# One attention and feed-forward kernel: the loads of q, k and v from the eighth pair on, moved from SyncE's queue to GpSimd's

## The chip, the cores and the metric

The kernel runs on one core of one Trainium2 chip. The metric is the device time of one execution in microseconds, given as the median of several runs. A core has five engines with an instruction queue each: TensorE (PE, matmuls; its weight loads are listed as PEld), VectorE (DVE), ScalarE (ACT), GpSimd (POOL) and SyncE (SP). Transfers (DMA) can be issued from the queues of SP, ACT and POOL; the core's 16 DMA engines carry them all. In the profile, SPq stands for SP's queue.

## What is computed

Attention over 8 batches of 8 heads with 1152 keys of 64 elements. The queries are first averaged in twos, so 576 are left. Behind it stands a feed-forward part without an activation function.

```python
batch, n_heads, seq, head_dim = (8, 8, 1152, 64)
...
q_pool = q.reshape(B, H, S // factor, factor, D).mean(axis=3)
scores = scale * np.matmul(q_pool, k.transpose(0, 1, 3, 2))
...
attn = np.exp(scores)
attn = attn / (np.sum(attn, axis=-1, keepdims=True) + 1e-09)
return np.matmul(attn, v).astype(np.float32)
...
a = x @ w1
b = x @ w2
h = a * b @ w3
return (h @ w_out).astype(np.float32)
```

Here x is the attention's result with the heads side by side: 4608 rows of 512. Inputs and output are float32. w1 and w2 are 512 x 1024, w3 is 1024 x 1024 and w_out is 1024 x 512.

## The kernel before

**Pairs.** Two heads of one batch form a pair; there are NP = 32 pairs, numbered from 0. For each pair the kernel loads k into kst, the queries into qst and a small rest of them into qtl (`load_kq`, L327, L330, L331), and v into vst (`load_v`, L337). Each of these tiles has two buffers, so the load of pair p needs the cast of pair p-2 to be done with its buffer.

**Casts, on POOL.** `cast_kq` turns k to float16 (L343) and adds neighbouring queries (L347, L349) into kq16, of which there are two. `cast_v` writes the values as float16 into vaug (L356), of which there are five.

**Turning.** Scores need keys and queries with the head's elements along the partitions. For pairs 1 to 7 TensorE turns kq16 (`transp_pe`, L371). From pair 8 on a DMA transpose on SP's queue does (`transp`, L363), into kqT, of which there are three. A DMA transpose on the same queue also turns the attention's results of pairs 8 to 31 (xb) into xT (`x_dma`, L473).

**Work on TensorE.** The scores of all pairs form one long row that is cut into 324 groups of 512 columns, three groups to a "visit". `scores` (L431) computes a group, and ACT takes the exponential (L436) into a ring. The product with the values (L459, L462) follows in units of 128 queries; DVE normalises (L483, L497). Between them stand matmuls of the feed-forward part as filling: first w3 times w_out, turned into one matrix T16 (L535, L544), then, as soon as 512 rows of x are there, the two projections (L566) and the product with T16 (L610). Its result goes through DVE (L620) into osb, of which there are three, and is stored to the output (`store`, L574, L578) from POOL's queue; in the tail of the kernel from SP's and ACT's. Each 512 rows make four such results.

**Order.** The order of instructions on each engine is the order in which the program names them; it is written out at build time. A planner (`_visits`) chooses what TensorE does between the scores of two visits, from a model of TensorE, ACT and DVE alone. While the scores of pair pn begin, the program names `transp(pn + 1)` and then `prepare(pn + 2)`. So on POOL the casts of pair p are followed by whatever `prepare(p)` issues from POOL, and then by the stores that come due.

**The loads' queues.** `prepare(p)` casts pair p's keys and queries and pair p-1's values, and then loads the values of pair p and the keys and queries of pair p+2. For p below 8 it issues these loads from POOL, from 8 on from SP. The loads before the first `prepare` go through several queues and the weights' loads through POOL's.

Of the kernel before, what the change touches and what calls it, by code (L numbers as in the profile page):

```python
# [255 lines left out]
def kernel(  # L256
# [11 lines left out]
    nc = tc.nc  # L268
# [55 lines left out]
    def load_kq(p, k_eng, q_eng):  # L324
        b, h0 = p // HP, 2 * (p % HP)
        kst = att.tile([128, 2, NJ * D], FP32, tag="kst")
        k_eng.dma_start(out=kst, in_=k[b, h0:h0 + 2].rearrange("u (p c) d -> p u (c d)", p=128))  # L327
        qst = att.tile([128, 2, QM * 2 * D], FP32, tag="qst")
        qtl = att.tile([QT, 2, 2 * D], FP32, tag="qtl")
        q_eng.dma_start(out=qst, in_=q[b, h0:h0 + 2, 0:QM * 256].rearrange("u (p c) d -> p u (c d)", p=128))  # L330
        q_eng.dma_start(out=qtl, in_=q[b, h0:h0 + 2, QM * 256:S].rearrange("u (p t) d -> p u (t d)", t=2))  # L331
        kq[p] = (kst, qst, qtl)

    def load_v(p, eng):
        b, h0 = p // HP, 2 * (p % HP)
        vst = att.tile([128, 2, NJ * D], FP32, tag="vst")
        eng.dma_start(out=vst, in_=v[b, h0:h0 + 2].rearrange("u (p c) d -> p u (c d)", p=128))  # L337
        vs[p] = vst

    def cast_kq(p):  # L340
        kst, qst, qtl = kq.pop(p)
        kq16 = kq16s[p % 2]
        nc.gpsimd.tensor_copy(out=kq16[:, 0:NJ].rearrange("p c u d -> p u c d"),  # L343
                              in_=kst.rearrange("p u (c d) -> p u c d", d=D))
        qv = qst.rearrange("p u (c t d) -> p u c t d", t=2, d=D)
        eng = nc.gpsimd
        eng.tensor_tensor(out=kq16[:, NJ:NJ + QM].rearrange("p c u d -> p u c d"),  # L347
                          in0=qv[:, :, :, 0], in1=qv[:, :, :, 1], op=ALU.add)
        eng.tensor_tensor(out=kq16[0:QT, NJ + QM], in0=qtl[:, :, 0:D], in1=qtl[:, :, D:2 * D], op=ALU.add)  # L349
        pairs[p] = kq16  # L350

    def cast_v(p):
        va = vaugs[p % NVA]
        if p < NVA:
            nc.gpsimd.memset(va[:, :, :, D:E1], 1.0 / SCL)
        nc.gpsimd.tensor_copy(out=va[:, :, :, 0:D], in_=vs.pop(p).rearrange("p u (c d) -> p u c d", d=D))  # L356
# [307 lines left out]
    def w3_load(r):  # L664
        nc.gpsimd.dma_start(out=w3c[r // 2][:, 2 * (r % 2):2 * (r % 2) + 2, :],
                            in_=moe_w3[256 * r:256 * r + 256, :].rearrange("(c p) f -> p c f", p=128))

    def w_load(dst, src):
        nc.gpsimd.dma_start(out=dst, in_=src.rearrange("(c p) f -> p c f", p=128))
# [24 lines left out]
    load_kq(3, nc.gpsimd, nc.gpsimd)  # L694

    def prepare(p):
        early = p < 8
        cast_kq(p)
        cast_v(p - 1)
        eng = nc.gpsimd if early else nc.sync  # L700
        load_v(p, eng)
        if p in (2, 3):
            w3_load(p)
        if p == 4:
            w_load(w1sb, moe_w1)
        if p == 5:
            w_load(w2sb, moe_w2)
        if p + 2 < NP:
            load_kq(p + 2, eng, eng)
# [13 lines left out]
    for c in range(B * Sq // CH):  # L723
        n = 0
        for b in range(B):
            for t in range(NT5):
                if xpos(b, t) < (c + 1) * CH and xpos(b, t) + (128 if t < QM else QT) > c * CH:
                    p = b * HP + HP - 1
# [44 lines left out]
    for vis in range(NVIS):  # L773
        if vis == T_START:
            queue.append(t_groups())
        for s in range(vis * VS, vis * VS + VS):
            pn = (s * G + G - 1) // FLAT
            if pn != seen:
                seen = pn
                if pn == 0:  # L780
                    first_turn(0, K0, turn_bank(), nc.scalar.copy)
                    first_turn(NJ, NJ + QM, avb.bitcast(FP16), nc.vector.tensor_copy, nc.scalar.copy)
                if NPE <= pn + 1 < NP:
                    transp(pn + 1)
                if 0 < pn < NP - 2:
                    prepare(pn + 2)
                elif pn + 2 == NP:
                    cast_v(NP - 1)
            scores(s)
            if s == 0:  # L790
                first_turn(NB - 1, NB, turn_bank(), nc.vector.tensor_copy)
        if vis == 0:
            first_turn(K0, NJ, turn_bank(), nc.vector.tensor_copy)
            prepare(2)
        for what in order[vis]:
            if what == "P":
                transp_pe(turn[vis].pop(0))
            elif what == "A":
                av_step()
            else:  # L800
                assert fill(what == "s")
# [67 lines left out]
```

## Time and profile before

| | us |
|---|---|
| median of three runs | 414.98 |
| lowest and highest of them | 414.73, 415.25 |
| span of the profiled execution | 414.1 |
| first score matmul | 7.1 |
| last score matmul ends | 346.6 |
| SP waiting before transposes of results (L473) for DVE | 49.1 + 44.3 in the two largest groups |
| vst, kst, qst: issue to landing from SP's queue, median | 4.9, 5.9, 7.2 |
| the same from POOL's queue | 7.2, 9.8, 10.4 |

The span runs from the first instruction to the end of the last one of the profiled execution; a run's time has a little around it. DMA time is read in two parts: the issue, which occupies the queue that issues it, and the landing, which is when its semaphore is complete. Packets of SP's queue (q1 in the profile) take 59.1% of the 16 DMA engines' span, those of POOL's queue (q0) 21.6%.

### The profile page before, as it was taken

The numbers are of one execution on the slowest core, as the hardware profiler recorded it, in microseconds if no ns is written. First come the engines' busy times: TensorE is split into PE (matmuls) and PEld (weight loads), VectorE is DVE, ScalarE is ACT, GpSimd is POOL, SyncE is SP. The second block draws the span as 40 slices with busy tenths as digits, with TensorE's granted clock in tenths as the row PEclk, the third lists the DMA queues.
The fourth block names the chain that finished last, engine by engine and source line by source line (L and its number), as shares of the span: only waits on it lengthen the run. The fifth ranks groups of instructions, "written<-read, shape, count | busy, mean of one in ns | idle before, by whom it ended". The sixth has DMA issues, their size and how long they took to land.

```text
span 414.1 us, 12744 instructions
## 1 busy us (share of the span) xinstructions
PE 399.9 (97%) x5337; PEld 246.9 (60%) x5337; DVE 205.5 (50%) x573; ACT 323.4 (78%) x353; POOL 167.6 (40%) x212
## 2 busy tenths in 40 slices
PE   3899999999999999999999999999999999999995
PEld 1477787565556655566556556655777655644442
DVE  1256665665356535554455436553556346744241
ACT  4878979898989998899999999999899986022321
POOL 4979976470655316504535155505532210010000
PEclk9999999999999999999999999999999999999999
DMA  8999999999799898959999999998975440030302
GB/s 263 210 320 289 269 286 312 348 247 265 185 238 252 221 286 278 242 70 278 273 264 280 264 252 270 292 260 163 303 207 121 85 90 15 16 114 2 101 0 108
DMA packets 90832, 86.34 MB, mean 209 GB/s; under 512 B 59664, under 2 KB 64272, under 8 KB 90768
## 3 DMA queue, kind: packets, MB, share of 16 engines
q1 hardware_dynamic: 81312, 58.80, 59.1%
q0 software_dynamic: 8880, 25.63, 21.6%
q10 hardware_dynamic: 576, 1.05, 0.8%
q8 instruction: 42, 0.69, 0.7%
q14 instruction: 22, 0.18, 0.1%
HBM read 67.11 MB, written 9.44 MB: 185 GB/s over the span
## 4 chain that ended last, share of the span: by engine, by line
PE 93%; ACT 2%; DMA 2%; DVE 1%; issue 1%; SPq 0%; POOL 0%; ACTq 0%
PE psc L431 20%; PE avb L462 17%; PE mot L566 16%; PE mo L566 15%; PE mo L610 11%; PE mot L610 5%; PE mo L544 3%; PE avb L459 3%; ACT ring L436 2%; PE ptk L371 2%; DMA kst<-in_k_dram 2%; DVE kqT L373 1%; PE mot L544 1%; PE mo L535 1%; PE mot L535 1%
## 5 line engine op out<-in xcount | busy, mean ns | idle before, releaser
L436 ACT ACTIVATE ring<-psc 128x1024 f16<-128x1024 f32 x324 | 308.3, 1025 | 33.8 <-PE psc L431 32.0
L462 PEld LDWEIGHTS <-ring 128*128 128x128 f16 x2304 | 84.4, 98 | 26.3 <-issue 7.1
L431 PE MATMUL psc<-kqT 64*128 64x512 f16 (+7 forms) x1152 | 96.2, 291 | 3.4 <-ACT ring L436 0.9
L462 PE MATMUL avb<-vaug,ring 128*128 128x65 f16 x2304 | 91.4, 193 | 0.0
L343 POOL CAST kq<-kst 128x1152 f16<-128x1152 f32 x31 | 35.7, 1150 | 74.3 <-DMA kqT<-kq 52.3
L431 PEld LDWEIGHTS <-kqT 64*128 64x128 f16 x1152 | 46.0, 95 | 31.0 <-issue 8.4
L578 POOL DMA_DIRECT2D out_dram<-osb x23 | 12.7, 551 | 101.6 <-DVE rzall L483 99.9
L610 PE MATMUL mo<-T,gT 128*128 128x512 f16 x192 | 45.6, 380 | 0.0
L566 PEld LDWEIGHTS <-w2sb 128*128 128x128 f16 x320 | 28.2, 98 | 28.3 <-issue 4.2
L566 PEld LDWEIGHTS <-w1sb 128*128 128x128 f16 x320 | 28.2, 98 | 27.7 <-issue 3.9
L610 PEld LDWEIGHTS <-gT 128*128 128x128 f16 x280 | 25.3, 98 | 32.2 <-issue 5.2
L483 DVE RECIPROCAL rzall<-avb 128x2 f32<-128x2 f32 x144 | 23.8, 165 | 37.0 <-PE avb L462 20.2
L566 PE MATMUL mot<-xT,w1sb 128*128 128x512 f16 (+2 forms) x172 | 41.1, 364 | 0.1
L620 DVE TENSOR_SCALAR osb<-mo 128x512 f32<-128x512 f32 x24 | 16.6, 692 | 48.5 <-PE mo L610 48.5
L347 POOL TENSOR_TENSOR kq<-qst 128x512 f16<-128x512 f32 x31 | 39.4, 1272 | 1.2 <-DMA qst<-in_q_dram 1.2
L566 PE MATMUL mot<-xT,w2sb 128*128 128x512 f16 (+2 forms) x156 | 38.0, 368 | 0.0
L356 POOL CAST vaug<-vst 128x1152 f16<-128x1152 f32 x32 | 36.6, 1143 | 2.6 <-DMA vst<-in_v_dram 2.5
L599 DVE TENSOR_TENSOR gT<-mot,asb 128x512 f16<-128x512 f32 x37 | 25.6, 692 | 22.0 <-PE mot L566 20.8
L599 DVE TENSOR_TENSOR gT<-mo,asb 128x512 f16<-128x512 f32 x35 | 24.2, 692 | 24.6 <-PE mo L566 24.4
L566 PE MATMUL mo<-xT,w2sb 128*128 128x512 f16 (+2 forms) x164 | 36.2, 349 | 0.0
L595 DVE COPY asb<-mo 128x512 f32<-128x512 f32 x32 | 22.1, 691 | 24.0 <-PE mo L566 23.7
L566 PE MATMUL mo<-xT,w1sb 128*128 128x512 f16 (+2 forms) x148 | 33.1, 351 | 0.0
(76 smaller groups left out, 287.4 us busy)
## 6 DMA issues: line engine op xcount, KB each, us to landing
vst<-in_v_dram SPq DMA_DIRECT2D x25, 576.0 KB, 4.9
kst<-in_k_dram SPq DMA_DIRECT2D x23, 576.0 KB, 5.9
qst<-in_q_dram SPq DMA_DIRECT2D x23, 512.0 KB, 7.2
out_dram<-osb POOLq DMA_DIRECT2D x23, 256.0 KB, 5.2
kst<-in_k_dram POOLq DMA_DIRECT2D x8, 576.0 KB, 9.8
qst<-in_q_dram POOLq DMA_DIRECT2D x8, 512.0 KB, 10.4
vst<-in_v_dram POOLq DMA_DIRECT2D x7, 576.0 KB, 7.2
w3c<-in_moe_w_dram POOLq DMA_DIRECT2D x4, 512.0 KB, 8.1
```

Of the source, the lines that this page charges most:

```text
L343: nc.gpsimd.tensor_copy(out=kq16[:, 0:NJ].rearrange("p c u d -> p u c d"), in_=kst.rearrange("p u (c d) -> p u c d", d=D))
L347: eng.tensor_tensor(out=kq16[:, NJ:NJ + QM].rearrange("p c u d -> p u c d"), in0=qv[:, :, :, 0], in1=qv[:, :, :, 1], op=ALU.add)
L356: nc.gpsimd.tensor_copy(out=va[:, :, :, 0:D], in_=vs.pop(p).rearrange("p u (c d) -> p u c d", d=D))
L431: nc.tensor.matmul(psc[:, u, f - s * G:f - s * G + ln], kT2[u * 64:u * 64 + 64, jt, :], qpT[u * 64:u * 64 + 64, i0:i0 + ln], start=True, s ...
L436: nc.scalar.activation(out=ring[:, :, r0:r0 + G], in_=psc, func=AF.Exp, bias=0.0, scale=SCALE)
L462: nc.tensor.matmul(avb[:, o + u * E1:o + u * E1 + E1], ring[:, u, c0:c0 + 128], va[:, u, jt, :], start=(jt == 0 and u == 0), stop=(jt == N ...
L483: nc.vector.reciprocal(out=rzall[:, i, :], in_=av[:, :, D:E1].rearrange("p u o -> p (u o)"))
L566: nc.tensor.matmul(pw[:, d0:d0 + n], wt[:, mc, ft * 128:ft * 128 + 128], xT[:, mc, a:a + n], start=(mc == 0 and d0 == 0), stop=(mc == NC - ...
L595: nc.vector.tensor_copy(out=t["a"], in_=pa)
L599: nc.vector.tensor_tensor(out=t["g"][:, ft, :], in0=pb, in1=t["a"], op=ALU.mult)
L610: nc.tensor.matmul(po, t["g"][:, ft, tt:tt + 128], T16[:, ft, :], start=(ft == 0), stop=(ft == NF - 1))
L620: nc.vector.tensor_scalar_mul(out=osb, in0=po, scalar1=1.0 / (SCL * SCL))
```

## The change

In `prepare`, the variable `early` goes, and all loads that this function issues go through POOL's queue.

```diff
     def prepare(p):
-        early = p < 8
         cast_kq(p)
         cast_v(p - 1)
-        eng = nc.gpsimd if early else nc.sync
+        eng = nc.gpsimd
         load_v(p, eng)
         if p in (2, 3):
             w3_load(p)
...
         if p + 2 < NP:
             load_kq(p + 2, eng, eng)
```

For p from 8 to 31 the load of the values, and for p from 8 to 29 the three loads of keys and queries of pair p+2, stand on POOL behind the casts of the same call. On SP's queue, after the loads of the start, the DMA transposes of kq16 and of xb are left, and the stores of the tail. Sizes, buffers and everything on TensorE, DVE and ACT stay as they are.

## The prediction

> **What bounds the kernel now.** I read the page's head first, then the stretch in which the changed loads act, then the waits, then the two queues that trade work.
>
> The page's first part, and the busy time of each engine from 90 to 346 us (from the first pair whose loads move until the last score matmul):
>
> ```profile
> span 414.1 us, 12744 instructions
> ...
> PE 399.9 (97%) x5337; PEld 246.9 (60%) x5337; DVE 205.5 (50%) x573; ACT 323.4 (78%) x353; POOL 167.6 (40%) x212
> ```
>
> ```profile
> 90.00:346.00 256.00, 255.68 (x3676) 158.34 (x3675) 130.04 (x364) 234.20 (x247) 97.96 (x113) 1.00 0.93 222
> ```
>
> In that stretch (columns: length, then busy us of PE, PEld, DVE, ACT, POOL; granted clock, DMA share, GB/s) TensorE is idle for 256.00 - 255.68 = 0.32 us, at a granted clock of 1.00. No load ends a TensorE wait there. So a better feeding of the data can win at most 0.3 us, and POOL, which gets the new work, is idle for 158 us.
>
> Whom the waits name, and the groups of POOL (busy us, mean ns of one, then idle time before it and its releaser):
>
> ```profile
> POOL out_dram L578 <- DVE rzall L483: 99.9, 18, 25.7
> POOL kq L343 <- DMA kqT<-kq: 52.3, 9, 12.6
> ```
>
> ```profile
> L347 POOL TENSOR_TENSOR kq<-qst 128x512 f16<-128x512 f32 x31 | 39.4, 1272 | 1.2 <-DMA qst<-in_q_dram 1.2
> L356 POOL CAST vaug<-vst 128x1152 f16<-128x1152 f32 x32 | 36.6, 1143 | 2.6 <-DMA vst<-in_v_dram 2.5
> L343 POOL CAST kq<-kst 128x1152 f16<-128x1152 f32 x31 | 35.7, 1150 | 74.3 <-DMA kqT<-kq 52.3 <-issue 11.8 <-PE ptk L371 5.7
> L349 POOL TENSOR_TENSOR kq<-qtl 64x128 f16<-64x128 f32 x31 | 14.0, 450 | 0.0
> L578 POOL DMA_DIRECT2D out_dram<-osb x23 | 12.7, 551 | 101.6 <-DVE rzall L483 99.9 <-DVE osb L620 1.7
> L330 POOL DMA_DIRECT2D qst<-in_q_dram x8 | 5.8, 728 | 0.0
> L327 POOL DMA_DIRECT2D kst<-in_k_dram x8 | 5.8, 726 | 0.0
> L337 POOL DMA_DIRECT2D vst<-in_v_dram x7 | 5.1, 726 | 0.0
> L331 POOL DMA_DIRECT2D qtl<-in_q_dram x8 | 4.9, 610 | 2.3 <-DMA wosb<-in_moe_w_out_dram 1.3 <-DMA w1sb<-in_moe_w_dram 1.0
> ```
>
> POOL mostly waits for results to store or for a transpose to have read the buffer that the next cast writes. The last four rows are the price of issuing on POOL what is to move.
>
> **The change part by part.** In the two programs' instruction orders, PE, DVE and ACT keep theirs. 90 issues leave SP and join POOL: 24 of vst (pairs 8 to 31) and 22 each of kst, qst and qtl (pairs 10 to 31).
>
> *POOL's time.* By the rows above a pair's four issues take 0.726 + 0.726 + 0.728 + 0.610 = 2.79 us. In all 24 x 0.726 + 22 x 2.064 = 62.8 us, so POOL goes from 167.6 to about 230 us (56%). A pair's casts take 1.150 + 1.272 + 0.450 + 1.143 = 4.02 us, and the 29 stores (15.9 us) come to 0.66 us a pair. A round is then 4.02 + 2.79 + 0.66 = 7.5 us. The pairs go by at (336.7 - 106.2) / 22 = 10.5 us, from the first score matmul of pair 9 to that of pair 31. POOL keeps 3 us a round. On the path that sets the end: 0.
>
> *What stands behind the new issues on POOL.* The next store or the next cast comes up to 2.8 us later. Here the cover counts, which I took pair by pair from the trace's landing times and first uses. The transposed keys kqT land 3.0 to 12.3 us before the first score matmul that reads them. The tightest are pairs 17, 18 and 19 (3.2, 3.0, 3.5 us). These three are held by SP's queue, not by POOL: the cast of pair 18 was done at 173.6, yet its transpose is issued at 187.74. The value tiles vaug are ready 18 to 36 us early.
>
> *SP's queue.* It loses 90 issues of 0.4 to 0.6 us, and what they blocked:
>
> ```profile
> 182.58 2.57 SPq L363 DMA_TRANSPOSE kqT<-kq  x1
> 185.24 0.54 SPq L337 DMA_DIRECT2D vst<-in_v_dram  x1
> 185.87 0.41 SPq L327 DMA_DIRECT2D kst<-in_k_dram  x1
> 186.38 0.42 SPq L330 DMA_DIRECT2D qst<-in_q_dram  x1
> 186.89 0.76 SPq L331 DMA_DIRECT2D qtl<-in_q_dram  x1
> 187.74 4.83 SPq L363 DMA_TRANSPOSE kqT<-kq  x1
> ```
>
> Pair 18's transpose waits here only for the issues before it; with these gone it follows pair 17's by about 185, 2.5 us earlier. Its 4.83 us (the shortest of the 24 took 1.53) I read as a ring still full of loads. All that is earlier feeds an engine with 0.3 us of idle time: 0 to -0.3 us, taken as 0.
>
> *The transfers.* Moved loads share the 16 DMA engines with the transposes as before, only from another ring. Landing on POOL's queue took a median of 7.2 us (vst), 9.8 (kst) and 10.4 (qst) against 4.9, 5.9 and 7.2 on SP's, but the POOL ones ran beside the weights, up to 1 MB each. The last set, clear of them (issued from 70.77), took 5.5, 6.7, 8.3 and 7.9 us. Bounds for the moved loads: 4.9 to 10.8 us for vst (slowest on POOL), 5.9 to 13.8 for kst. I take the last set, the nearest in kind. A kst or qst is issued two rounds ahead, 2 x 10.5 - 6.8 = 14 us before its cast: covered at all but the slowest qst seen (14.7). A vst is issued one round ahead; the round holds while it lands within 10.5 - 1.1 = 9.4 us: covered, except at the bound.
>
> *Placing POOL's issue against DVE.* The moved issues took 0.71 to 0.75 us each for kst in the first 75 us, when DVE worked most. In the stretch in question no DVE instruction takes over 0.69 us, so if each issue waited for a whole one, a round is 7.5 + 4 x 0.69 = 10.2 us, still under 10.5.
> The Trainium skill speaks against the change here: "SBUF — State Buffer", section "A bandwidth-pool intuition that's wrong", has a GpSimd-issued DMA of about 0.62 us take about 3.1 us beside a VectorE copy that holds the port the two share. By that figure a round would be some 17 us and the kernel some 150 us slower, an estimate from that page alone; the trace, with 31 load issues all near their usual length, does not agree.
>
> **Sum:** span 414.1 + 0. The median of the three runs (414.98) lies 0.9 us above this execution's span and moves with it: 415.0 us, own range 414.4 to 415.6 (0.3 us of idle time and the runs' spread of 0.5).
>
> **The rivals.**
>
> *A, slower: POOL's own load loop becomes the bound.* Place: from a vst issue through its landing to the cast at L356 and the next vst issue, all on POOL in order. It decides once vst lands later than 9.4 us. At the slowest 10.8 a round is 10.8 + 1.1 = 11.9 us: 24 x 1.4 = 34 us, less some 9 us of kqT cover, about 440. For it: three of seven POOL vst took 8.7 us or more. Against: these ran beside weights; the one clear set took 5.5.
>
> *B, slower by little: a store late enough to hold its buffer.* osb has three buffers and each group of output rows writes four. Only the group stored from 193.81 has casts just before it (to 191.1); the new issues fill 191.1 to 193.9, and its first store queues behind 1.7 MB of loads. It landed at 200.18; the fourth osb is written at 202.25. If it lands 9 to 10.4 us after the loads' last issue, plus a little for itself, that is 203 to 205. DVE is then 1 to 3 us late, of which 1.1 us (osb's end at 202.94 to the next matmul on that bank at 204.01) is free: 415.0 to 416.8.
>
> *C, slower: the transposes lose their place.* In one ring an earlier transpose precedes later loads; in two rings they mix. If pair 17's transpose, issued at 182.6 because of DVE and not of the loads, landed after the longest time seen (11.2 us), it would be at 193.8 against a first use at 190.4: +3.4, so 418.4. The same place has xT for the chunk projected from 204.0: landed 204.5, read by the fourth matmul at 204.66. Against: both sat behind loads in one ring before.
>
> *D, slower: the issue itself is blocked by DVE* (above): over 10.5 us a round needs more than 0.75 us lost at each issue; at 1 us each, (11.5 - 10.5) x 24 = 24 us, about 439.
>
> *E, faster:* 0.3 us idle is all there is. A gain over 0.8 us needs TensorE itself to run faster while fewer loads sit in SP's ring: nothing in the rows speaks for it. 414.0 at most.
>
> That the change doesn't move the loads is excluded by the instruction orders.
>
> **How the numbers follow.** Forecast 0.74, A 0.05, B 0.09, C 0.08, D 0.01, E 0.03. About 0.2% (0.8 us) is what this measurement can tell from no change. Half of B stays within it: same 0.74 + 0.05 = 0.79, slower 0.04 + 0.05 + 0.08 + 0.01 = 0.18, faster 0.03. The range takes the forecast's own low end, and reaches past B, 416.8, to 417.0; C, A, D and E lie outside (0.17).
>
> **What would show it.** Right: POOL near 230 us busy, TensorE's idle time from 90 to 346 under 1 us, SP's kqT transposes issued in nearer 1.5 than 3.6 us, kqT of pairs 17 to 19 earlier. Wrong: a wait of score matmuls for the kqT transposes (C), of POOL's L356 for vst in most rounds (A), of DVE's L620 for a store (B), or POOL issues of over 1 us (D).

## The result, and the profile after

The changed kernel takes a median of 438.87 us (four runs, 434.31 to 447.81), beside 414.94 us for the kernel before on the same chip. The ratio is 1.0535, with a 95% interval of 1.0502 to 1.0567: slower by 5.4%, where 415.0 us was forecast. The ratio, like each one below, leaves out runs over 1.5% above the fastest of the same kernel, here the one of 447.81. The runs also differ by 13.5 us among themselves; those of the kernel before lie within 0.5 us.

The head of the page of the profiled execution (438.53 us), with the row of granted clock and that of GB/s from its 40 slices of 10.9 us:

```profile
span 436.8 us, 12622 instructions
...
PE 405.6 (93%) x5337; PEld 249.5 (57%) x5337; DVE 205.7 (47%) x573; ACT 323.5 (74%) x353; POOL 229.4 (53%) x302
...
PEclk9999999999999999999689999999988999999999
...
GB/s 276 266 302 327 290 297 253 220 222 216 249 300 210 228 248 245 297 120 237 119 161 232 252 226 238 253 271 223 251 208 127 93 87 38 14 110 1 98 0 102
```

The loss of 22.7 us of span has two parts. TensorE's time without work grew from 414.1 - 399.9 = 14.2 to 436.8 - 405.6 = 31.2 us, by 17.0. Its busy time grew by 405.6 - 399.9 = 5.7 us for the same 5337 matmuls: the clock row falls to 6 and 8 tenths in places. POOL is busy for 229.4 us, where about 230 was worked out. In the slice from 207.5 to 218.4 us the DMA engines move only 119 GB/s, although transfers are waiting, as the stretch below shows.

Who waited, in the list of waits (us in total, times, longest):

```profile
POOL kq L343 <- DMA kqT<-kq: 55.7, 8, 13.8
...
PE psc L431 <- DMA kqT<-kq: 10.1, 3, 6.1
...
DVE osb L620 <- DMA out_dram<-osb: 8.6, 1, 8.6
...
PE avb L462 <- DVE xb L497: 7.4, 2, 6.5
POOL vaug L356 <- DMA vst<-in_v_dram: 5.9, 6, 2.3
```

The two PE rows hold 10.1 + 7.4 = 17.5 us, which is about the new idle time (17.0). The first is a wait for turned keys. In the second TensorE waits for DVE's L497, which in turn stood behind L620 and its wait for a store.

The list of transfers (line, queue, count, KB each, median us from issue to landing) of the changed kernel:

```profile
vst<-in_v_dram POOLq DMA_DIRECT2D x31, 576.0 KB, 6.1
kst<-in_k_dram POOLq DMA_DIRECT2D x30, 576.0 KB, 7.7
qst<-in_q_dram POOLq DMA_DIRECT2D x30, 512.0 KB, 9.2
out_dram<-osb POOLq DMA_DIRECT2D x23, 256.0 KB, 8.1
```

and its transposes there, then the stores and the same two in the list of the kernel before:

```profile
kqT<-kq SPq DMA_TRANSPOSE x24, 9.7
xT<-xb SPq DMA_TRANSPOSE x24, 6.9
```

```profile
out_dram<-osb POOLq DMA_DIRECT2D x23, 256.0 KB, 5.2
...
kqT<-kq SPq DMA_TRANSPOSE x24, 6.6
xT<-xb SPq DMA_TRANSPOSE x24, 4.8
```

In the median the loads landed near what was forecast for them (5.5, 6.7 and 8.3): the moved ones alone have 6.2, 7.1 and 8.5, the slowest of them 14.5, 15.2 and 17.5. What nobody moved got late: kqT from 6.6 to 9.7 us, with a longest of 28.9 instead of 11.2 us, xT from 4.8 to 6.9, the stores from 5.2 to 8.1.

**One stretch, step by step.** POOL, SP's queue and the end of DVE's wait around the first large hole, from the timeline (start us, us, then in brackets the idle time before it and its releaser). POOL:

```profile
190.92 1.15 POOL L343 CAST kq<-kst 128x1152 f16<-128x1152 f32 x1 [9.86 <-DMA kqT<-kq]
...
194.73 0.72 POOL L337 DMA_DIRECT2D vst<-in_v_dram  x1
...
196.89 0.60 POOL L331 DMA_DIRECT2D qtl<-in_q_dram  x1
197.48 1.12 POOL L578 DMA_DIRECT2D out_dram<-osb  x2
...
208.92 0.60 POOL L331 DMA_DIRECT2D qtl<-in_q_dram  x1 [1.80 <-DMA qtl<-in_q_dram]
...
224.68 1.15 POOL L343 CAST kq<-kst 128x1152 f16<-128x1152 f32 x1 [13.79 <-DMA kqT<-kq]
```

SP's queue:

```profile
195.71 6.60 SPq L363 DMA_TRANSPOSE kqT<-kq  x1
212.18 1.19 SPq L473 DMA_TRANSPOSE xT<-xb  x1
213.47 11.09 SPq L363 DMA_TRANSPOSE kqT<-kq  x1
```

DVE and PE:

```profile
209.32 0.69 DVE L620 TENSOR_SCALAR osb<-mo 128x512 f32<-128x512 f32 x1 [8.65 <-DMA out_dram<-osb]
...
210.47 1.15 PE L462 MATMUL avb<-vaug,ring 128*128 128x65 f16 x18 [6.48 <-DVE xb L497]
```

The cast of pair 19 and the first of these stores in the kernel before:

```profile
187.24 1.15 POOL L343 CAST kq<-kst 128x1152 f16<-128x1152 f32 x1 [12.64 <-DMA kqT<-kq]
...
193.81 0.57 POOL L578 DMA_DIRECT2D out_dram<-osb  x1 [2.68 <-DVE rzall L483]
```

The transpose of pair 17 landed at 190.8. The cast of pair 19, which writes the buffer that this transpose read, so began at 190.92; before, the same cast began at 187.24. Behind it on POOL stand the pair's loads and then the first store, issued at 197.48 though its data were there at 194.0. It landed at 209.22, 11.7 us later (before: 6.4 us). Only then could DVE write the fourth osb, at 209.32 instead of 202.25, and TensorE stood still for 6.48 us. The transpose of pair 19, whose issue began at 195.71, landed at 224.6, after 28.9 us; the score matmuls had waited 3.69 us for it by then, and POOL's next cast 13.79. A third hole of 6.09 us, for the transpose of pair 28, ends at 325.5.

Windows of the same stretch (length, then busy us and counts of PE, PEld, DVE, ACT, POOL; granted clock, DMA share, GB/s):

```profile
206.00:210.00 4.00, 0.00 (x0) 0.00 (x0) 0.68 (x2) 0.51 (x1) 1.73 (x3) 0.69 1.43 165
210.00:214.00 4.00, 3.53 (x50) 2.15 (x51) 1.48 (x6) 0.00 (x0) 0.58 (x1) 0.50 1.34 94
214.00:218.00 4.00, 4.00 (x62) 2.39 (x58) 2.40 (x8) 2.86 (x3) 0.00 (x0) 0.96 1.04 120
```

The DMA engines count as fully busy and yet move 94 to 165 GB/s. TensorE, back at work at 210.47, has half the clock for four microseconds: that is where busy time grows. The clock record has 0.50 from 207.5 to 214.4, and the hole had begun at 204.0. The Trainium skill, "TensorE: Matmul & The Clock Gate", section "Part 1: The HAM clock gate (the "warmup" mystery)", lets the clock fall to a half after an idle window of about 3.4 us; the 0.50 behind this hole agrees.

Packets by the time at which they start, summed from the trace in steps of 2 us, show what the busy engines do (on SP's ring the small packets of qtl are left out):

```
kernel before                              changed kernel
from   256-byte      loads on SP's         from   256-byte      data on POOL's
us     transposes    ring, GB/s            us     transposes    ring, GB/s
186    439           135                   204    315           190
188      0           350                   206    359           164
190     12           355                   208    277            77
192   1482            12                   210    113            38
194    298           189                   212    120           120
196      0           334                   214     53            99
                                           216    179           111
                                           218      0           304
```

Before, one ring mostly made them take turns: at 188 and 190 nearly loads alone at 350 GB/s, at 192 nearly transposes alone, some 1500 packets in 2 us. In the changed kernel both are in flight together, and from 208 to 218 neither comes near its rate: at most 277 packets and 120 GB/s. At 218 no packet of a transpose starts, though pair 19's has not landed, and the loads are back at 304 GB/s; most of the transposes' packets that are left follow from 222 on.

Over the whole stretch from 90 to 346 us the difference is one of degree. Steps of 1 us in which over 20 packets of transposes start beside over 30 GB/s of other data number 54 before and 81 after. In these steps 359 packets of transposes start per us before and 213 after, beside 150 and 175 GB/s.

### The profile page after: what moved, and what is told of

It reads as the page before. It is cut to its first block, busy times and chain, and to the rows that moved or that the text cites. A ratio compares the mean times of both kernels' runs of the same rounds, so it can differ in the third digit from the quotient of the medians.

```text
span 436.8 us, 12622 instructions
## 1 busy us (share of the span) xinstructions
PE 405.6 (93%) x5337; PEld 249.5 (57%) x5337; DVE 205.7 (47%) x573; ACT 323.5 (74%) x353; POOL 229.4 (53%) x302
## 4 chain that ended last, share of the span: by engine, by line
PE 79%; DMA 16%; ACT 2%; DVE 1%; issue 1%; ACTq 0%; POOL 0%; SPq 0%
PE psc L431 17%; DMA kqT<-kq 15%; PE mot L566 14%; PE avb L462 14%; PE mo L566 12%; PE mo L610 8%; PE mot L610 4%; PE mo L544 3%; PE avb L459 2%; ACT ring L436 2%; PE ptk L371 2%; DMA qst<-in_q_dram 1%; DVE kqT L373 1%; PE mot L544 1%; PE mo L535 1%
## 5 line engine op out<-in xcount | busy, mean ns | idle before, releaser
L431 PE MATMUL psc<-kqT 64*128 64x512 f16 (+7 forms) x1152 | 97.4, 292 | 13.7 <-DMA kqT<-kq 10.1
L462 PEld LDWEIGHTS <-ring 128*128 128x128 f16 x2304 | 85.4, 98 | 33.8 <-issue 14.5
L620 DVE TENSOR_SCALAR osb<-mo 128x512 f32<-128x512 f32 x24 | 16.6, 692 | 56.7 <-PE mo L610 44.9
L566 PE MATMUL mot<-xT,w1sb 128*128 128x512 f16 (+2 forms) x172 | 42.2, 372 | 0.0
L356 POOL CAST vaug<-vst 128x1152 f16<-128x1152 f32 x32 | 36.6, 1143 | 6.6 <-DMA vst<-in_v_dram 5.9
L566 PE MATMUL mo<-xT,w2sb 128*128 128x512 f16 (+2 forms) x164 | 37.9, 362 | 0.0
L566 PE MATMUL mo<-xT,w1sb 128*128 128x512 f16 (+2 forms) x148 | 34.0, 358 | 0.0
```

Of the source, the lines that this page charges most:

```text
L431: nc.tensor.matmul(psc[:, u, f - s * G:f - s * G + ln], kT2[u * 64:u * 64 + 64, jt, :], qpT[u * 64:u * 64 + 64, i0:i0 + ln], start=True, s ...
L462: nc.tensor.matmul(avb[:, o + u * E1:o + u * E1 + E1], ring[:, u, c0:c0 + 128], va[:, u, jt, :], start=(jt == 0 and u == 0), stop=(jt == N ...
L566: nc.tensor.matmul(pw[:, d0:d0 + n], wt[:, mc, ft * 128:ft * 128 + 128], xT[:, mc, a:a + n], start=(mc == 0 and d0 == 0), stop=(mc == NC - ...
```

## The experiments

Ratios are to the kernel before on the same chip, with a 95% interval where the runs gave one.

**POOL's time alone.** The kernel before, with as much work on POOL as the new issues take, at their place, and no load moved:

```diff
+    idle16 = const.tile([128, 1152], FP16)
+    nc.vector.memset(idle16, 0.0)
...
+        if not early:
+            for n in (1152, 1152, 384):
+                nc.gpsimd.tensor_copy(out=idle16[:, 0:n], in_=idle16[:, 0:n])
```

> The kernel before (loads of q, k and v on SP), with three copies of a scratch tile on POOL at the place where the changed kernel issues its loads, some 2.8 us a pair from pair 8 on, so that POOL is as busy as after the change but issues nothing more. Theory 1 (loads in POOL's ring mixing with the DMA transposes in SP's ring is what costs): no change, 414.5 to 415.8 us. Theory 2 (POOL's issue time makes the casts late): as slow as the changed kernel, 430 to 440 us. Theory 3 (the stores stand behind the loads in POOL's ring and hold osb): no change.

415.31 us, ratio 0.9984 (0.9961 to 1.0008), with POOL at 233.9 us busy. The later casts and stores that this brings cost nothing; the loss is in the transfers and in their order on POOL's queue.

**No DMA transposes.** TensorE turns all keys, queries and results, once with the loads on SP's queue and once with them on POOL's:

```diff
-    XD = 8
+    XD = 32
...
-    NPE = 8
+    NPE = 32
```

> The kernel before with all turns on TensorE (NPE and XD from 8 to 32), so that no DMA transpose is left; loads on SP as before. Reference for the next kernel. TensorE gets 24 more groups of 14 transposes (0.94 us each) and 96 small ones: all theories expect 440 to 455 us.

> The changed kernel (loads on POOL) with all turns on TensorE, no DMA transpose left. Theory 1: equal to the kernel with all turns on TensorE and loads on SP, within 0.3%, since nothing is left to mix with. Theory 2: slower than it by some 3 to 5%, since POOL's issue time is all there. Theory 3: slower than it by 1 to 2%, from waits of L620 for a store.

444.81 and 444.78 us, ratios 1.0698 (1.0665 to 1.0732) and 1.0699 (1.0663 to 1.0734). Both pay for 432 more matmuls (TensorE 427.4 us busy in both), and the queue of the loads makes no difference to the time. The transfers of the second of them, loads on POOL, in the view used above:

```profile
vst<-in_v_dram POOLq DMA_DIRECT2D x31, 576.0 KB, 4.4
kst<-in_k_dram POOLq DMA_DIRECT2D x30, 576.0 KB, 6.3
qst<-in_q_dram POOLq DMA_DIRECT2D x30, 512.0 KB, 7.4
out_dram<-osb POOLq DMA_DIRECT2D x21, 256.0 KB, 5.3
```

The same loads and stores land 1.4 to 2.8 us sooner than in the changed kernel. So, as far as these two show, the move costs time only where transposes run beside it. Two reservations. With TensorE busier, the pairs go by more slowly and each load has a little more time. And the move makes transfers later here too: with the loads on SP's queue kst landed in 4.0 us and the stores in 3.4, with them on POOL's in 6.3 and 5.3. Of the 2.9 us by which the stores got later in the changed kernel, 1.9 are so seen without any transposes; here they cost nothing.

**A fourth osb.** The changed kernel with four buffers where there were three:

```diff
-                osb = msb.tile([128, dm], FP32, tag="osb", bufs=3)
+                osb = msb.tile([128, dm], FP32, tag="osb", bufs=4)
...
-                osb = msb.tile([128, dm], FP32, tag="osb", bufs=3)
+                osb = msb.tile([128, dm], FP32, tag="osb", bufs=4)
```

> The changed kernel with four buffers for osb in place of three, so that the fourth result of a group needs no store of its own group. The changed kernel lost 7.4 us to such waits in its profile (0.95 at 159.8 and 6.48 at 210.5) and 10.1 us to late kqT transposes, and its granted clock fell after the long ones. Theory 1: the waits for kqT stay, 425 to 434 us. Theory 3: most of the loss goes, 415 to 420 us. Theory 2: 425 to 438 us.

Four runs from 423.38 to 461.13 us (median 448.81): too far apart for a verdict. The profile is of the fastest, and tells which waits were left:

```profile
PE psc L431 <- DMA kqT<-kq: 5.3, 1, 5.3
...
PE mot L566 <- DMA xT<-xb: 0.8, 1, 0.8
```

In it TensorE no longer waits behind a store, as expected, and still waits 5.3 us for a transpose, so a late transpose doesn't need a late store. That a fourth buffer makes the kernel faster is not shown.

**The loads on ScalarE's queue**, in the kernel before, keys and queries one pair ahead instead of two:

```diff
-        eng = nc.gpsimd if early else nc.sync
+        eng = nc.gpsimd if early else nc.scalar
...
-        if p + 2 < NP:
+        if early:
             load_kq(p + 2, eng, eng)
+        elif 10 <= p + 1 < NP:
+            load_kq(p + 1, eng, eng)
```

> The kernel before with the moved loads on ACT's queue in place of SP's, a second hardware ring, POOL issuing none of them; keys and queries are loaded one pair ahead, not two, so that ACT need not wait for the cast just named. ACT, 90% busy, gets some 1.7 us of issues a pair and may slow the kernel by itself (up to 20 us), so the answer is in the transposes: issue to landing of kqT, median 6.6 us before and 10.1 after the change. Theory 1a (any second ring beside the transposes' own stretches them): median 9 us or more. Theory 1b (only POOL's software-made descriptors do): median under 8 us.

443.67 us (two runs, 439.57 and 447.76; the profile is of the second), but for a reason of its own: TensorE waited 16.8 + 5.0 us for ScalarE's exponentials, which the issues delay. No score matmul waited for a transpose, and kqT landed in a median of 6.3 us. A control was needed for the shorter look-ahead, the changed kernel, its loads on POOL, with the same look-ahead:

```diff
-        if p + 2 < NP:
+        if p < 8:
             load_kq(p + 2, eng, eng)
+        elif 10 <= p + 1 < NP:
+            load_kq(p + 1, eng, eng)
```

> The changed kernel with keys and queries loaded one pair ahead on POOL's queue, as in the kernel that had its loads on ACT's queue: the control for that one. If it is POOL's ring that stretches the transposes, kqT issue to landing has a median of 9 us or more here against 6.5 there; if it was the place of the loads, under 8 us here too. Time 425 to 460 us, since the casts wait for later loads.

471.06 us (two runs), ratio 1.1351 (1.1274 to 1.1429), most of it four waits behind stores (31.9 us); kqT there took a median of 5.6 us, with a longest of 15.7. So the 6.3 us with the loads on ScalarE's queue is no evidence on its ring: the shorter look-ahead alone shortens the median.

**Loads only after the turn.** In the changed kernel POOL reads one element of the keys turned last ahead of the loads, so that they start when that transpose has landed:

```diff
+    seen16 = const.tile([1, 1], FP16)
...
+        if p > NPE:
+            nc.gpsimd.tensor_copy(out=seen16, in_=pairs[p - 1][0][0:1, 0, 0:1])
         eng = nc.gpsimd
```

> The changed kernel; before each set of loads POOL reads one element of the kqT last turned, so that the loads start only when that transpose has landed, and mix with the next one less. The next cast needs that landing anyway. Theory 1: most of the loss goes, 415 to 422 us, kqT issue to landing near 7 us. Rivals that put the loss on POOL's queue (order or time): as slow as the changed kernel or slower, 434 to 450 us, since POOL only waits more.

447.54 us (four runs, 441.39 to 460.29): no gain. The waits say why (its line numbers are one higher):

```profile
DVE osb L621 <- DMA out_dram<-osb: 26.9, 3, 12.7
...
PE avb L463 <- DVE xb L498: 20.3, 3, 10.6
...
PE psc L432 <- DMA kqT<-kq: 2.2, 1, 2.2
```

With this wait the transposes have the median of the kernel before again (6.6 us, the longest 17.2), and TensorE's wait for them falls from 10.1 to 2.2 us. It doesn't keep the packets apart altogether: both kinds still start together in 69 of the 256 steps of 1 us counted above. But the new wait stands on POOL, and the stores stand behind it: 20.3 us behind three late stores. That was not in the expectation, and led to the next two.

**The stores on SP's queue**, in the changed kernel, in the changed kernel with the wait of the last experiment, and in the kernel before:

```diff
-                    store(nc.gpsimd, c * CH + tt, osb)
+                    store(nc.sync, c * CH + tt, osb)
```

> The changed kernel with the stores of osb on SP's queue, behind no load and no cast, ahead of the tail too. Theory A (two separate costs: transposes stretched by loads in POOL's ring, and stores that stand behind casts and loads on POOL and hold osb): the waits of L620 for a store go, those for kqT stay, 420 to 434 us. Theory B (only the stretched transposes; the late stores follow from them): 434 us and more. Theory C (only the stores): 415 to 417 us.

> Both repairs on the changed kernel: loads wait for the last transpose of kqT to land, and stores go through SP's queue. Theory A: nearly all of the loss goes, 415 to 419 us. Theory B: as with the wait alone, 430 us and more, since stores on SP stand behind transposes. Theory C: 415 to 419 us too, and told from A by the kernel with the stores alone moved.

> The kernel before with its stores on SP's queue, behind the loads and transposes there: what the place of the stores is worth by itself. All theories: 414.5 to 418 us if a store there lands within the 9 us that three osb buffers leave; more if it stands behind a transpose that waits.

429.09 us, ratio 1.0338 (1.0308 to 1.0368); 423.05 us, 1.0173 (1.0119 to 1.0227); 416.49 us, 1.0036 (1.0016 to 1.0057). By the ratios the stores' place is worth 5.35 - 3.38 = 2.0 of the 5.4 percent, and both repairs together 5.35 - 1.73 = 3.6. The first two still wait for keys now and then (4.5 and 3.5 us), the second also 2.0 us for turned results, and in the first one wait of L620 for a store is left (4.8 us), where none was expected. Neither of these two reaches the kernel before.

**One part of the loads at a time.** In the kernel before, only the values on POOL, then only keys and queries:

```diff
-        load_v(p, eng)
+        load_v(p, nc.gpsimd)
```

```diff
-            load_kq(p + 2, eng, eng)
+            load_kq(p + 2, nc.gpsimd, nc.gpsimd)
```

> A part of the change: only the values' load on POOL from pair 8 on (0.58 of 1.73 MB a pair); keys and queries stay on SP. Theory 1: part of the mixing and so part of the loss, kqT issue to landing between 6.6 and 10.1 us, 415 to 428 us.

> The other part: keys and queries on POOL from pair 10 on (1.15 MB a pair), the values' load stays on SP. Theory 1: more mixing than with the values alone, kqT issue to landing 8 to 10 us, 420 to 440 us.

428.8 us, ratio 1.0308 (1.0218 to 1.0398), and 416.5 us, 1.0053 (1.0009 to 1.0096; ten runs, 415.55 to 428.68). Keys and queries, two thirds of the bytes, were expected to cost more, and cost less; no score matmul waits for a transpose there. So the bytes on POOL's ring alone do not set the loss. Waits of the kernel with the values alone on POOL, and a window of it:

```profile
POOL vaug L356 <- DMA vst<-in_v_dram: 58.4, 17, 11.8
...
DVE osb L620 <- DMA out_dram<-osb: 5.2, 1, 5.2
...
PE psc L431 <- DMA kqT<-kq: 4.5, 2, 4.2
```

```profile
116.00:120.00 4.00, 4.00 (x55) 2.34 (x51) 2.60 (x8) 3.38 (x5) 0.77 (x2) 1.00 1.16 97
```

A vst issued at 111.4 and two stores of 112 to 113 each took 17 us to land, while the engines, busy throughout, moved 97 GB/s. Values are loaded one pair ahead and their cast stands in POOL's order, so a late vst stops POOL, its stores and the next keys' cast. Keys and queries are loaded two pairs ahead and can be late without that; this reading of the difference was not tested by itself. Moved together, L356 waits only 5.9 us, so this is not the main path in the changed kernel. The two parts alone come to 3.1 + 0.5 = 3.6 percent and together to 5.4: the parts don't add up.

**The values on ScalarE's queue** instead of POOL's:

```diff
-        load_v(p, eng)
+        load_v(p, nc.gpsimd if early else nc.scalar)
```

> The kernel before with the values' load of pairs 8 to 31 on ACT's queue, at the same place in the program as in the kernel that had it on POOL's (that one: 428.8 us, kqT issue to landing 8.7 us in the median). ACT gets one issue of some 0.4 us a pair and needs no long wait for it. If any second ring beside the transposes' own makes them late: 420 us and more, with TensorE waiting for kqT. If it takes POOL's ring, or POOL's place in the order: 415 to 417 us, no such wait.

418.9 us, ratio 1.0098 (1.0063 to 1.0133), against 428.8 with the values on POOL's. Another second ring goes with a loss as well, though a third as large. What makes it up is not shown: no wait of TensorE for a transpose or a store is named in this profile, and ScalarE has 24 more issues. The edit also takes the issue out of POOL's order, so this run doesn't tell the kind of ring from the place of the issue.

The kernels side by side; kqT is issue to landing, median (by the list of transfers) and longest of the 24. Where an expectation above names a median of 10.1 us for the changed kernel or 8.7 for the values on POOL, the list has 9.7 and 8.5.

| kernel | ratio | kqT median | longest |
|---|---|---|---|
| before | 1 | 6.6 | 11.2 |
| before, stores on SP | 1.0036 | 6.4 | 9.5 |
| keys and queries on POOL | 1.0053 | 7.8 | 12.0 |
| values on ScalarE's queue | 1.0098 | 7.2 | 12.0 |
| changed, after the turn, stores on SP | 1.0173 | 7.5 | 15.3 |
| values on POOL | 1.0308 | 8.5 | 18.2 |
| changed, stores on SP | 1.0338 | 8.0 | 13.9 |
| changed | 1.0535 | 9.7 | 28.9 |

Where kqT takes longer the kernel mostly takes longer too, though not in strict order. In the steps of 1 us in which both kinds start, counted as above, 346 packets of transposes start per us with keys and queries on POOL, 313 with the values on ScalarE's queue and 276 with them on POOL's, between the 359 before and the 213 after. After the turn with the stores left on POOL (447.54 us, median 6.6) and one pair ahead (471.06 us, 5.6) stand outside this row, because their time goes to late stores.

## Why the prediction was wrong

**What bounds it, and POOL's time: right.** TensorE had 0.3 us to win and nothing was won. POOL came to 229.4 us against 230, the issues took 0.61 to 0.73 us in the mean, and the same time on POOL without the loads cost nothing. D, an issue blocked by DVE, is excluded by those issue times. The figure weighed there, from the Trainium skill, "SBUF — State Buffer", section "A bandwidth-pool intuition that's wrong", holds beside a VectorE copy that has the shared port; that case is not seen in these issue times.

**SP's queue: wrong.** The transposes' issue was to fall from 3.6 toward 1.5 us, since the loads ahead of them in the ring were thought to hold it. With the loads gone the median is 4.4 us and the longest 11.1. Of pairs 17 to 19, whose kqT was to come earlier, only pair 18's did (193.3 us for 197.0); pair 17's landed at 190.8 for 187.1 and pair 19's at 224.6 for 208.6.

**"The transfers": the step that failed.** It said that moved loads share the 16 DMA engines with the transposes "as before, only from another ring". The ring was the point. In one ring a transpose and the loads behind it mostly took turns (the table of packets above); in two they run at once for longer, and where they meet both crawl. The loads' landing was taken from the last set at the start of the kernel, and no DMA transposes ran there. For the loads that figure was still close in the median, though the slowest (14.5 and 15.2 us for vst and kst) lie outside the bounds of 10.8 and 13.8. What it left out is what the loads do to the transposes and the stores, and that is the loss: the transfers were put at 0 and brought 17.5 us of waits of TensorE. The Trainium skill, "DMA: Bandwidth & Descriptors", section "Issuing engines are not separate DMA queues", has transfers of all issuing engines interleave on the same 16 engines, and lets the choice of the issuer matter for the issue time only. The two kernels without DMA transposes, equal to 0.03 us, agree in their time, though not in their landings (kst 4.0 and 6.3 us); beside transposes the choice of queue cost 5.4%.

**C: the right mechanism, mis-sized and misplaced.** It had "in two rings they mix", and priced it at one place, pair 17, with the longest landing then seen: 11.2 us, +3.4. Pair 17 cost 0.33 us. Pairs 19 and 28 cost 3.69 and 6.09, with a landing of 28.9 us. A longest time seen in a regime that the change ends was no bound for the regime that it begins.

**B: the right place, too small.** The group stored from 194 did hold osb. B took the loads to start at 191.1 and the fourth osb to be written at 203 to 205; it was written at 209.32. About 3.6 us of this is the loads' own start, at 194.73: C's late transpose of pair 17 had held the cast before them. The rest is the store's landing, 11.7 us. The rivals were priced one by one, but one feeds the other.

**A: not the main path.** vst landed in a median of 6.1 us, under the 9.4 from which A decides, and L356 waits 5.9 us in all. With the values alone on POOL it does decide now and then (58.4 us of POOL's time).

**Not in the sum at all:** the 5.7 us by which TensorE's busy time grew behind the holes, at a lower granted clock.

**Open.** Why single packets wait when the two kinds meet (up to 4.5 us for one of 256 bytes, 3.1 before) is not shown by any run. The queue also changed the packets, which the prediction did not reckon with: in the traces kst and vst move in packets of 2304 bytes from SP's and ScalarE's queues and of 4608 from POOL's, qst in 2048 and 4096. No run changes the queue and holds the size; size alone is not the answer, since keys and queries, two thirds of these larger packets' bytes, cost 0.5%. Nor is it settled whether POOL's ring is worse than another second ring, or only the place of the issue in POOL's order. A deeper look-ahead for the values was not tried. No kernel run here beats the kernel before.

## What to carry to other kernels

Before a load is moved to another queue, ask what its old queue kept in order: here one ring had DMA transposes and loads mostly take turns and kept the stores from standing behind loads, and giving that up cost 5.4%. Price a transfer only by rows in which the same neighbours run, and price the unmoved transfers too. A store that shares an in-order queue with casts and their waits needs either more buffers than results or a queue of its own.

## What the runs showed of the hardware

DMA transposes alone ran at some 1500 packets of 256 bytes in 2 us (2096 in the changed kernel, from 188) and loads alone at 350 GB/s; mixed from two rings, both fell, at worst to 113 packets in 2 us and 38 GB/s, while the engines' busy share stayed above 1. The same load moves in packets of 2304 bytes from SP's queue and of 4608 from POOL's. A busy DMA share alone so does not tell how much is moved. And runs of one such kernel scatter: 434.31 to 447.81 us as changed, 423.38 to 461.13 with a fourth osb, where four of the kernel before lay from 414.73 to 415.25.
